# Folding a softmax scale, evicting two PSUM banks in one copy, and warming TensorE: one change of five parts to a packed attention and MLP kernel

## The chip, the cores and the metric

The kernel runs on one core of a Trainium2 chip. The metric is device time in microseconds (us), the median of several executions. The profile is taken in one execution; its span is 1.7 to 2.1 us shorter than the device time of that execution, so spans are compared with spans and times with times.

Engine names in the profile: PE is the matmul engine (TensorE), PEld its weight loads, DVE is VectorE, ACT is ScalarE, POOL is GpSimd, SP is the engine whose queue issues the stores. To evict means to copy a result from PSUM, where TensorE writes it, to SBUF. A "wall" is here an event, such as the landing of a load, before which a stage cannot begin.

Tile names: `a` or `a1` holds the weights of the first softmax, `a1T` their transpose, `a2u` the exponentials of the second softmax, `lns` the logarithms of its sums, `a2n` its normalised weights, `cosT` the cosine and `gT` the gated result.

## The reference

Two attentions follow one another, then an MLP with a cosine gate. There are 8 batches, 8 heads, 576 positions, a head size of 64, 32 "packed" queries, a model width of 512 and an inner width of 2048.

```python
def sm_attn(qq, kk, vv):
    s = scale * np.matmul(qq, kk.transpose(0, 1, 3, 2))
    a = softmax(s)                      # max subtracted, 1e-9 added to the sum
    return np.matmul(a, vv)
p_packed = sm_attn(p, k, v)             # 32 packed rows per head
out = sm_attn(q, p_packed, p_packed)    # every query looks at the 32 packed rows
x = out as (batch*576, 512)
h = x @ w_in
return (h * np.cos(h)) @ w_out
```

## The kernel before

The kernel never forms `x`. Because `x = A2 @ p_packed`, it multiplies the packed rows by `w_in` first (`PPW`, 256 rows by 2048 columns per batch, in four tiles of 512 columns) and then computes `h` as `A2 @ PPW`. The first softmax is not normalised when it is computed: its sums (the key sums) become a factor `r1` per packed row, which is applied when `PPW` is evicted from PSUM.

```python
def ppw(b, n, engs, pool=A):                    # tile n of packed-times-w_in
    ...
    t = psa(); ps = [t[:, 0, :], t[:, 1, :]]    # two PSUM banks of one tile
    for x in range(4):
        for y in range(2):
            nc.tensor.matmul(ps[y][32 * x:32 * x + 32, :], ppT[b % 2][r, 2 * x + y, :], w_in_bf[...])
    for y in range(2):                          # engs is (V, ACT) nearly everywhere
        dst = PPW[b][:, y, n * 512:(n + 1) * 512]
        if engs[y] is ACT:
            ACT.activation(out=dst, in_=ps[y], func=AF.Copy, scale=r1[b][:, y:y + 1])
        else:
            V.tensor_scalar(out=dst, in0=ps[y], scalar1=r1[b][:, y:y + 1], op0=ALU.mult)

def normalise(b):                               # second softmax: a2n = a2u / sum
    for y in range(2):
        ACT.activation(out=lns[b][:, y], in_=lns[b][:, y], func=AF.Exp, scale=-1.0)
    for y in range(2):
        V.tensor_tensor(out=a2n[b][:, y], in0=a2u[b][:, y], in1=lns[b][:, y], op=ALU.mult)

def h_mm(b, fc):                                # one of 16 chunks of h (128 columns)
    ps = psa()                                  # pool A: three tiles of two banks
    for y in range(2):
        for e in range(2):
            nc.tensor.matmul(ps[:, e, 0:HS], PPW[b][:, y, ...], a2n[b][:, y, ...], start=(y == 0), stop=(y == 1))
    ACT.activation(out=csv, in_=ps[:, :, 0:HS], func=AF.Sin, bias=pihalf)
    # rest(): DVE multiplies psum by the cosine and writes gT
```

Each engine does its instructions in the order in which the program gives them. The order is made by hand. In `ppw`, batch 0 is an exception: its halves go each into a PSUM tile of its own (pool `O`). `fill(n)` puts n matmuls of the previous batch's output product (128x512, the "filler") into TensorE's order wherever the batch's own work would leave it waiting. `slot(s, ...)` runs the 16 h chunks of batch s, and between them the pack product `pp` and the four `ppw` tiles of the next batch.

```python
for s in range(2, B):
    set_filler(s - 1)
    s2(s); fill(7)                       # query scores, exponentials
    s1(s + 1); xbar(...); a1_xbar(s + 1) # key scores of the next batch; a1 transposed by DMA
    fill(3); sums2(s, 0); fill(4); sums2(s, 1); normalise(s); fill(11)
    slot(s, front(s + 1, 4))             # pp at chunk 4, ppw at 7, 9, 11, 13
```

Batch 0 has no filler. Batch 1's transposes are done by TensorE, and their PSUM results are copied by DVE, ACT and DVE in turn (those of `a1` by DVE and ACT). The loads are all issued at the start, in the order keys, values, queries of batch 0, `w_in` (two pieces), the pack rows of batches 1 to 7, `w_in` (two pieces), `w_out` (four pieces), keys, values, queries of batch 1, and so on.

The softmax here doesn't subtract the row's maximum and nothing guards it: scores larger than these inputs give would overflow.

## Time and profile before

The time was 278.81 us (278.59 to 280.82, 3 runs). The table cuts the span by the loads of ACT's function tables, which mark the stages well: the exponential set is loaded before each batch's softmax, the sine set before its h chunks. "Period" is from one batch's exponential load to the next.

| stage | span before, us | what fills it |
|---|---|---|
| start to batch 1's exponential set | 38.96 | batch 0 alone, no filler |
| from there to batch 1's sine set ("stage 2") | 20.33 | attention of batch 1, with batch 0's filler |
| from there to batch 2's exponential set ("slot 1") | 23.96 | h of batch 1, six `ppw` tiles |
| periods of batches 2, 4, 6 | 29.71, 30.80, 29.71 | 80 filler matmuls each |
| periods of batches 3, 5 | 29.36, 28.92 | 64 filler matmuls each |
| batch 7 and the rest | 45.15 | h of batch 7, 80 output matmuls, last stores |

Busy shares of the whole span, and the row of TensorE's granted clock in 40 slices (9 is full speed), from the page of the kernel before:

```profile
PE 244.3 (88%) x1996; PEld 130.9 (47%) x1996; DVE 158.3 (57%) x257; ACT 191.1 (69%) x296; POOL 53.2 (19%) x67
...
PEclk9999999999999999999999999999999999999997
```

TensorE is busy 88% of the span, but a mean over such different stages says little. The busy time by stage says more (columns: stretch, its length, then busy us and instruction count of PE, PEld, DVE, ACT, POOL, then clock, DMA share, GB/s). The four rows are stage 2, slot 1, and batches 3 and 6:

```profile
core 0: us, PE busy (x) PEld busy (x) DVE busy (x) ACT busy (x) POOL busy (x), PEclk, DMA share, GB/s
38.96:59.29 20.33, 18.54 (x236) 10.69 (x234) 11.02 (x21) 13.65 (x26) 6.99 (x7) 1.00 1.19 181
59.29:83.25 23.96, 18.10 (x172) 9.34 (x172) 17.26 (x27) 17.48 (x27) 3.47 (x6) 1.00 0.89 133
...
112.96:142.32 29.36, 26.95 (x237) 13.94 (x236) 17.70 (x28) 22.97 (x36) 6.38 (x7) 1.00 0.85 151
...
202.04:231.75 29.71, 29.02 (x228) 15.21 (x234) 17.46 (x28) 23.14 (x36) 4.09 (x4) 1.00 0.35 78
```

In batch 6 TensorE is busy 98% of the time, in batch 3 92%, and in slot 1 only 18.1 of 24.0 us, with DVE and ACT no fuller. Slot 1 is held by an order of waits and not by one engine. The group list shows which (columns: line, engine, operation, out<-in, shapes, count | busy us, mean ns | idle us before it <- what ended it):

```profile
L188 ACT ACTIVATE PPW<-psA,r 128x512 bf16<-128x512 f32 x28 | 19.2, 687 | 18.4 <-DVE PPW L190 18.4
...
L190 DVE TENSOR_SCALAR PPW<-psA,r 128x512 bf16<-128x512 f32 x28 | 20.8, 744 | 0.6 <-PE psA L183 0.5
...
L214 DVE TENSOR_TENSOR a2n<-a2u,lns 128x576 bf16<-128x576 bf16 x16 | 11.4, 755 | 12.8 <-ACT lns L212 12.8
```

ACT sat idle 18.4 us in front of its 28 halves of the eviction, and each time DVE's half ended the idle time. The two halves, which were meant to run side by side, ran one after the other. The totals of the waits (who waited for whom: us in all, times, longest):

```profile
ACT PPW L188 <- DVE PPW L190: 18.4, 28, 1.6
...
PE psA L226 <- DVE a2n L214: 3.8, 9, 2.2
...
PE psA L160 <- DMA a1T<-a: 2.9, 3, 1.4
```

One turn of this in slot 1, in the timeline (start us, duration, engine, instruction, idle before and its cause):

```profile
77.81 0.76 DVE L233 TENSOR_TENSOR gT<-psA,cosT 128x576 bf16<-128x576 f32 x1 [0.72 <-ACT cosT L230]
...
78.48 0.74 DVE L190 TENSOR_SCALAR PPW<-psA,r 128x512 bf16<-128x512 f32 x1
...
79.26 0.69 ACT L188 ACTIVATE PPW<-psA,r 128x512 bf16<-128x512 f32 x1 [0.58 <-DVE PPW L190]
79.85 0.73 ACT L230 ACTIVATE cosT<-psA,pihalf 128x576 bf16<-128x576 f32 x1
80.00 0.65 PE L226 MATMUL psA<-a2n,PPW 128*128 128x288 bf16 x4 [0.51 <-ACT PPW L188]
```

DVE multiplies gT (77.81), then evicts its half (78.48), then ACT evicts its half (79.26), then ACT makes the next cosine (79.85), on which the next gT waits; TensorE's next h chunk (80.00) waits for ACT's half as well, because it needs the PSUM tile. One such turn takes 2.8 us for two h chunks.

The start of the kernel, in the timeline, and the landing time of the load that was issued at 19.29 (last column of the DMA view: us from issue to landing):

```profile
7.78 2.10 PE L102 MATMUL psA<-ident,kbf 96*128 96x96 bf16 x24 [3.83 <-DMA kbf<-in_k_dram]
...
19.29 0.79 POOL L84 DMA_DIRECT2D kbf<-in_k_dram  x1 [2.16 <-PE psA L124]
...
23.75 5.50 PE L226 MATMUL psA<-a2n,PPW 128*128 128x288 bf16 x24 [2.18 <-DVE a2n L214]
...
39.82 1.46 PE L102 MATMUL psA<-ident,kbf 96*128 96x96 bf16 x24
```

```profile
kbf<-in_k_dram POOLq DMA_DIRECT2D x1, 576.0 KB, 20.2
```

Two things are read here. The first 24 h matmuls of 288 columns took 5.50 us, 229 ns each; in the raw trace they start 240 ns apart up to 28.2 us and, within a chunk, 122 ns apart later. TensorE ran at half speed until then, although the clock row shows 9 throughout: the trace's first clock record is one of full speed at 28.30 us, and the row counts time without a record as full speed. And the keys of batch 1, which the transposes at 39.82 need, landed at 19.29 + 20.2 = 39.5 us. The transposes show no wait for them: batch 0's own chain still ended last, with the keys 0.3 us ahead.

### The profile page before, as it was taken

The page shows a single profiled execution, that of the slowest core. Times are in us where ns is not written, and L with a number is a line of the kernel's source. Part 1 is how long each engine was busy: PE and PEld are TensorE (multiplying, and loading weights), DVE is VectorE, ACT ScalarE, POOL GpSimd, SP SyncE. Part 2 cuts the span into 40 slices and gives each one's busy share as a digit, 9 for nine tenths or more (in the row PEclk, how much of TensorE's full clock was granted, in tenths as well). Part 3 has the DMA queues.
Part 4 walks back from the last instruction along what each step waited for, and adds up shares of the span by engine and source line. Part 5 has one row for each costly group of instructions (what it writes and reads, how often), then busy time and mean ns, then how long its engine had stood idle before and what let it go on. Part 6 is the DMA issues. An engine that isn't in the chain of part 4 may idle for free.

```text
span 276.9 us, 5007 instructions
## 1 busy us (share of the span) xinstructions
PE 244.3 (88%) x1996; PEld 130.9 (47%) x1996; DVE 158.3 (57%) x257; ACT 191.1 (69%) x296; POOL 53.2 (19%) x67
## 2 busy tenths in 40 slices
PE   0786889977879999998899999989999999999992
PEld 0563455444424655455445555455445544565440
DVE  2348995447771677456663677267726765587100
ACT  1347984696679766995789577977797678876000
POOL 8432002610404120403031300411040000000000
PEclk9999999999999999999999999999999999999997
DMA  7999999999299999299919894989264202111222
GB/s 98 204 224 206 206 206 157 199 153 177 23 202 182 193 156 175 62 191 163 216 45 170 166 220 90 145 193 160 59 132 94 52 29 62 43 40 38 76 76 77
DMA packets 62759, 37.09 MB, mean 134 GB/s; under 512 B 35488, under 2 KB 58016, under 8 KB 62736
## 3 DMA queue, kind: packets, MB, share of 16 engines
q0 software_dynamic: 23168, 18.81, 45.1%
q1 hardware_dynamic: 39568, 17.96, 30.9%
q8 instruction: 15, 0.25, 0.4%
q14 instruction: 8, 0.07, 0.1%
HBM read 37.22 MB, written 9.44 MB: 169 GB/s over the span
## 4 chain that ended last, share of the span: by engine, by line
PE 54%; ACT 18%; DVE 16%; DMA 6%; issue 4%; SPq 0%; ACTq 0%; POOLq 0%
PE ot L261 28%; PE psA L226 14%; DVE gT L233 6%; ACT cosT L230 5%; DVE PPW L190 5%; DMA a1T<-a 4%; ACT PPW L188 3%; DVE a2n L214 3%; PE psA L160 3%; PE psA L102 2%; DMA kbf<-in_k_dram 2%; PE psA L124 2%; ACT lns L206 2%; ACT lns L212 2%; PE psA L204 2%
## 5 line engine op out<-in xcount | busy, mean ns | idle before, releaser
L261 PE MATMUL ot<-w_out_bf,gT 128*128 128x512 bf16 x512 | 132.6, 380 | 0.0
L233 DVE TENSOR_TENSOR gT<-psA,cosT 128x576 bf16<-128x576 f32 x128 | 95.7, 755 | 41.6 <-ACT cosT L230 40.2
L230 ACT ACTIVATE cosT<-psA,pihalf 128x576 bf16<-128x576 f32 x128 | 93.5, 741 | 20.4 <-PE psA L226 19.0
L226 PE MATMUL psA<-a2n,PPW 128*128 128x288 bf16 x512 | 86.2, 291 | 10.8 <-DVE a2n L214 3.8
L226 PEld LDWEIGHTS <-PPW 128*128 128x128 bf16 x512 | 50.5, 99 | 51.5 <-issue 19.2
L261 PEld LDWEIGHTS <-gT 128*128 128x128 bf16 x512 | 46.7, 98 | 42.3 <-issue 6.9
L237 POOL COPY joint<-gT 128x512 bf16<-128x512 bf16 x16 | 9.7, 612 | 124.8 <-DVE gT L233 124.8
L188 ACT ACTIVATE PPW<-psA,r 128x512 bf16<-128x512 f32 x28 | 19.2, 687 | 18.4 <-DVE PPW L190 18.4
L75 ACT COPY osb<-ot 128x512 f32<-128x512 f32 x18 | 10.5, 581 | 16.1 <-PE ot L261 16.0
L190 DVE TENSOR_SCALAR PPW<-psA,r 128x512 bf16<-128x512 f32 x28 | 20.8, 744 | 0.6 <-PE psA L183 0.5
L77 DVE COPY osb<-ot 128x512 f32<-128x512 f32 x18 | 12.3, 682 | 11.6 <-PE ot L261 11.6
L214 DVE TENSOR_TENSOR a2n<-a2u,lns 128x576 bf16<-128x576 bf16 x16 | 11.4, 755 | 12.8 <-ACT lns L212 12.8
L77 POOL COPY vp<-vbf 96x3072 bf16<-96x3072 bf16 x6 | 16.5, 2749 | 0.0
L261 PE MATMUL ot<-w_out_bf,joint 128*128 128x512 bf16 x64 | 16.5, 380 | 0.0
L139 DVE RECIPROCAL r<-sums 128x2 f32<-128x2 f32 x8 | 1.3, 166 | 22.9 <-ACT a L133 22.9
L170 ACT CAST ppT<-psA 64x128 bf16<-64x128 f32 x16 | 4.2, 260 | 11.6 <-DVE ppT L166 9.8
L196 ACT ACTIVATE a2u<-psA,rs 128x576 bf16<-128x576 f32 x16 | 11.0, 737 | 1.2 <-PE psA L124 1.1
L183 PE MATMUL psA<-w_in_bf,ppT 64*32 64x512 bf16 x224 | 11.5, 386 | 0.3 <-DVE gT L233 0.2
L160 PE MATMUL psA<-a1T,vp 96*128 96x64 bf16 x192 | 7.5, 199 | 4.5 <-DMA a1T<-a 2.9
L133 ACT ACTIVATE a<-psA 128x576 bf16<-128x576 f32 x16 | 10.3, 652 | 1.7 <-PE psA L124 1.7
L206 ACT ACTIVATE lns<-psA 128x576 f32<-128x576 f32 x16 | 10.4, 659 | 1.2 <-PE psA L204 0.7
L84 POOL DMA_DIRECT2D kbf<-in_k_dram x8 | 6.3, 787 | 21.6 <-PE psA L102 18.6
(54 smaller groups left out, 154.5 us busy)
## 6 DMA issues: line engine op xcount, KB each, us to landing
kbf<-in_k_dram POOLq DMA_DIRECT2D x8, 576.0 KB, 11.5
vbf<-in_v_dram POOLq DMA_DIRECT2D x8, 576.0 KB, 7.0
qbf<-in_q_dram POOLq DMA_DIRECT2D x8, 576.0 KB, 9.4
out_dram<-osb SPq DMA_DIRECT2D x24, 192.0 KB, 2.5
out_dram<-osb SPq DMA_DIRECT2D x24, 128.0 KB, 2.4
w_in_bf<-in_moe_w_in_dram POOLq DMA_DIRECT2D x4, 512.0 KB, 15.4
w_out_bf<-in_moe_w_out_dram POOLq DMA_DIRECT2D x4, 512.0 KB, 20.4
out_dram<-osb SPq DMA_DIRECT2D x24, 64.0 KB, 2.1
```

Source lines behind the costliest of these rows:

```text
L77: eng.tensor_copy(out=out, in_=in_)
L160: nc.tensor.matmul(ps[:, 0, hp * 64:(hp + 1) * 64], vp[b][:, c, hp * 128:(hp + 1) * 128], a1T[b][0:TP, :, j, 32 * hp:32 * hp + 32], start= ...
L183: nc.tensor.matmul(ps[y][32 * x:32 * x + 32, :], ppT[b % 2][r, 2 * x + y, :], w_in_bf[r, x, n * 512:(n + 1) * 512], start=True, stop=True)
L188: ACT.activation(out=dst, in_=ps[y], func=AF.Copy, scale=r1[b][:, y:y + 1])
L190: V.tensor_scalar(out=dst, in0=ps[y], scalar1=r1[b][:, y:y + 1], scalar2=None, op0=ALU.mult)
L196: ACT.activation(out=a2u[b][:, y].rearrange("p (e x) -> p e x", e=2), in_=ps[y][:, :, 0:HS], func=AF.Exp, scale=rs1[b][:, y:y + 1])
L206: ACT.activation(out=lns[b][:, y].rearrange("p (e x) -> p e x", e=2), in_=ps[:, :, 0:HS], func=AF.Ln)
L214: V.tensor_tensor(out=a2n[b][:, y], in0=a2u[b][:, y], in1=lns[b][:, y], op=ALU.mult)
L226: nc.tensor.matmul(ps[:, e, 0:HS], PPW[b][:, y, fc * 128:(fc + 1) * 128], a2n[b][:, y, e * HS:(e + 1) * HS], start=(y == 0), stop=(y == 1))
L230: ACT.activation(out=csv, in_=ps[:, :, 0:HS], func=AF.Sin, bias=pihalf)
L233: V.tensor_tensor(out=gT[b][:, fc, :].rearrange("p (e x) -> p e x", e=2), in0=ps[:, :, 0:HS], in1=csv, op=ALU.mult)
L261: nc.tensor.matmul(ps, w, w_out_bf[:, fc, :], start=(fc == 0), stop=(fc == NFC - 1))
```

## The change

The intent was to take work off DVE and ACT in the slots and to keep TensorE busy and warm. It has five parts: (1) the key-sum scale `r1` moves from the eviction of `PPW` to the query normalisation, so that a `PPW` tile (two banks) can be evicted in one copy, by DVE and ACT in turn, with batch 0's tiles now in the shared pool too (the result is the same, since `r1` belongs to the packed row over which `h` sums); (2) 25 warm-up matmuls on zeros in batch 0; (3) the transposes of batch 1, the first ones of batch 2 and those of `a1` in batch 0 evicted by DVE alone; (4) other positions: fill counts 8, 4, 5, 13 in place of 7, 3, 4, 11, the pack product at chunk 5 in place of 4, two of batch 2's `ppw` tiles from slot 1 to slot 2, the packing of `p` in two parts; (5) the last output chunk in two halves, stored from two queues.

```diff
-    def ppw(b, n, engs, pool=A):
+    def ppw(b, n):
...
-        for y in range(2):
-            dst = PPW[b][:, y, n * 512:(n + 1) * 512]
-            if engs[y] is ACT:
-                ACT.activation(out=dst, in_=ps[y], func=AF.Copy, scale=r1[b][:, y:y + 1])
-            else:
-                V.tensor_scalar(out=dst, in0=ps[y], scalar1=r1[b][:, y:y + 1], scalar2=None, op0=ALU.mult)
+        copy((V, ACT)[n % 2], PPW[b][:, :, n * 512:(n + 1) * 512], ps)
...
-            V.tensor_tensor(out=a2n[b][:, y], in0=a2u[b][:, y], in1=lns[b][:, y], op=ALU.mult)
+            V.scalar_tensor_tensor(out=a2n[b][:, y], in0=a2u[b][:, y], scalar=r1[b][:, y:y + 1],
+                                   in1=lns[b][:, y], op0=ALU.mult, op1=ALU.mult)
...
+    def warm(n):
+        for _ in range(n):
+            nc.tensor.matmul(wps, wz[:, 0:128], wz, start=True, stop=True)
...
-            copy((V, ACT)[y], t[0:TP, y]..., ps[0:TP, 0, 0:C * 128])      # a1 of batches 1, 2 (and 0)
+            copy(V, t[0:TP, y]..., ps[0:TP, 0, 0:C * 128])
-            copy(ACT if i == 1 else V, t[:, 8 * i:8 * i + 8]..., ps[:, 0, 0:8 * TP])
+            copy(engs[i], ...)                                            # engs=(V, V, V); batch 0 (V, ACT, V)
...
+    warm(7)
     dup_p(0, 2)
     pack_p(0, 1)
-    pe_T("k", 0)
+    warm(9)
+    pe_T("k", 0, (V, ACT, V))
...  # warm(3) before a1 of batch 0, warm(6) after its normalise
-    for n in range(4):
-        for fc in range(4 * n, 4 * n + 4):
-            h_mm(0, fc)()
-            if fc == 4 * n + 1 and n in (1, 2):
-                ppw(0, n + 1, (V, ACT), O)
+    for fc in range(NFC):
+        h_mm(0, fc)()
+        if fc in (2, 6):
+            ppw(0, 2 + fc // 4)
+        if fc == 10:
+            pack_p(1, 3)
...
-    slot(1, [(1, ppw(1, 2)), (5, ppw(1, 3))] + front(2, 6), ...)          # abridged
+    slot(1, [(1, pw(1, 2)), (4, pw(1, 3)), (7, lambda: pp(2)), (9, lambda: pack_p(3, B)),
+             (11, pw(2, 0)), (14, pw(2, 1))], ...)
...
-        fill(7)
+        fill(8)
...
-        fill(3)
+        fill(4)
         sums2(s, 0)
-        fill(4)
+        fill(5)
         sums2(s, 1)
         normalise(s)
-        fill(11)
+        fill(13)
...
-        slot(s, front(s + 1, 4) if nxt else [], [])
+        pieces = [(1, pw(2, 2)), (4, pw(2, 3))] if s == 2 else []
+        if nxt:
+            pieces += [(5, lambda: pp(s + 1))] + [(8 + 2 * n, pw(s + 1, n)) for n in range(4)]
+        slot(s, pieces, [])
...
+    tail_chunk(B - 1, 4)      # last 128 rows: two halves of 256 columns, stores on SP and ACT queues
```

More of the change, by code (lines that the diff above doesn't have):

```diff
@@ L69 @@
     srcs = {"k": k, "q": q, "v": v}
-    bf, vp, xT, a1T, r1, rs1 = {}, {}, {}, {}, {}, {}
+    bf, vp, xT, a1T, sums1, r1, rs1 = {}, {}, {}, {}, {}, {}, {}
     a2u, lns, a2n, PPW = {}, {}, {}, {}
@@ L93, in xbar, with pe_T @@
         nc.sync.dma_start_transpose(out=t, in_=bf[n, b].rearrange("p h x -> p (h x)"))
-    def pe_T(n, b):
+    def pe_T(n, b, engs=(V, V, V)):
         t = xT[n, b] = att_pool.tile([128, H * 3, TP], BF16, name=n + "T", tag=n + "T")
@@ L103, in pe_T @@
                                     ident[0:TP, 0:TP])
-            copy(ACT if i == 1 else V, t[:, 8 * i:8 * i + 8].rearrange("p a x -> p (a x)"),
+            copy(engs[i], t[:, 8 * i:8 * i + 8].rearrange("p a x -> p (a x)"),
                  ps[:, 0, 0:8 * TP])
@@ L136, in s1, with recips @@
                 func=AF.Exp, scale=scale, accum_out=sm[:, y:y + 1])
+        sums1[b] = sm
+    def recips(b):
         r1[b] = small.tile([128, 2], FP32, name="r1")
         rs1[b] = small.tile([128, 2], FP32, name="rs1")
-        V.reciprocal(r1[b], sm)
+        V.reciprocal(r1[b], sums1[b])
         V.tensor_scalar(out=rs1[b], in0=r1[b], scalar1=scale, scalar2=None, op0=ALU.mult)
@@ L152, in a1_pe @@
                 nc.tensor.transpose(ps[0:TP, 0, c * 128:(c + 1) * 128], a1[b % 2][:, y, c, 0:TP], ident)
-            copy((V, ACT)[y], t[0:TP, y].rearrange("p c x -> p (c x)"), ps[0:TP, 0, 0:C * 128])
+            copy(V, t[0:TP, y].rearrange("p c x -> p (c x)"), ps[0:TP, 0, 0:C * 128])
     def pp(b):
@@ L170, in pp @@
             ACT.copy(out=t[z, :, y, :], in_=pv[r, :, y, :])
-    def ppw(b, n, engs, pool=A):
+    def ppw(b, n):
         if b not in PPW:
             PPW[b] = ppw_pool.tile([128, 2, DF], BF16, name="PPW", tag="PPW")
-        if pool is O:
-            ps = [O.tile([128, 512], FP32, name="ppw", tag="ot") for _ in range(2)]
-        else:
-            t = psa()
-            ps = [t[:, 0, :], t[:, 1, :]]
+        ps = psa()
         for x in range(4):
@@ L182, in ppw @@
                 r = slice(64 * y, 64 * y + 64)
-                nc.tensor.matmul(ps[y][32 * x:32 * x + 32, :], ppT[b % 2][r, 2 * x + y, :],
+                nc.tensor.matmul(ps[32 * x:32 * x + 32, y, :], ppT[b % 2][r, 2 * x + y, :],
                                  w_in_bf[r, x, n * 512:(n + 1) * 512], start=True, stop=True)
-        for y in range(2):
-            dst = PPW[b][:, y, n * 512:(n + 1) * 512]
-            if engs[y] is ACT:
-                ACT.activation(out=dst, in_=ps[y], func=AF.Copy, scale=r1[b][:, y:y + 1])
-            else:
-                V.tensor_scalar(out=dst, in0=ps[y], scalar1=r1[b][:, y:y + 1], scalar2=None, op0=ALU.mult)
+        copy((V, ACT)[n % 2], PPW[b][:, :, n * 512:(n + 1) * 512], ps)
     def s2(b):
@@ L254, in pieces_of, with n_chunks, tail_chunk @@
         return res
+    def n_chunks(b):
+        return 5 if b % 2 and b < B - 1 else 4
+    def tail_chunk(b, c):
+        osb = o_pool.tile([128, DM], FP32, name="osb")
+        for i in range(2):
+            cols = slice(i * 256, i * 256 + 256)
+            ps = O.tile([128, 256], FP32, name="ot", tag="ot")
+            for fc in range(NFC):
+                nc.tensor.matmul(ps, joint[b // 2][:, fc, :], w_out_bf[:, fc, cols],
+                                 start=(fc == 0), stop=(fc == NFC - 1))
+            copy((ACT, V)[i], osb[:, cols], ps)
+            for (a, z, rows), q in zip(pieces_of(b, c), (nc.sync, nc.scalar)):
+                q.dma_start(out=rows[:, cols], in_=osb[a:z, cols])
     def out_gen(b):
-        for c in range(5 if b % 2 else 4):
+        for c in range(n_chunks(b)):
             ps = O.tile([128, DM], FP32, name="ot", tag="ot")
@@ L275, in set_filler @@
         filler[0] = out_gen(b)
-        filler[1] = 16 * (5 if b % 2 else 4)
+        filler[1] = 16 * n_chunks(b)
     def fill(n):
@@ L294, in dup_p, with load_w_in, load_w_out @@
             V.tensor_copy(out=p_bf[:, a:b, t, :], in_=p_raw[:, a:b, :])
+    def load_w_in(n):
+        G.dma_start(out=w_in_bf[:, :, n * 512:(n + 1) * 512],
+                    in_=moe_w_in.rearrange("(a p) n -> p a n", p=128)[:, :, n * 512:(n + 1) * 512])
+    def load_w_out(n):
+        G.dma_start(out=w_out_bf[:, n * 4:(n + 1) * 4, :],
+                    in_=moe_w_out.rearrange("(a p) n -> p a n", p=128)[:, n * 4:(n + 1) * 4, :])
+    def dup_p(a, b):
+        for t in range(2):
+            V.tensor_copy(out=p_bf[:, a:b, t, :], in_=p_raw[:, a:b, :])
+    def warm(n):
+        for _ in range(n):
+            nc.tensor.matmul(wps, wz[:, 0:128], wz, start=True, stop=True)
     nc.sync.dma_start(out=p_raw[:, 0:2, :], in_=p_rows[:, 0:2, :])
@@ L313 @@
     load("q", 2)
+    wz = const.tile([128, 512], BF16, name="wz")
+    wps = O.tile([128, 512], FP32, name="wps", tag="ot")
+    V.memset(wz, 0.0)
     ACT.preload_act_table_set(EXP_SET)
@@ L320 @@
         V.memset(t[:, :, :, TP:128], 0.0)
+    warm(7)
     dup_p(0, 2)
     pack_p(0, 1)
-    pe_T("k", 0)
+    warm(9)
+    pe_T("k", 0, (V, ACT, V))
     s1(0)
     permute_v(0, V)
+    warm(3)
     a1_pe(0)
+    recips(0)
     pp(0)
-    pe_T("q", 0)
+    pe_T("q", 0, (V, ACT, V))
     s2(0)
-    ppw(0, 0, (V, V), O)
+    ppw(0, 0)
     sums2(0, 0)
     sums2(0, 1)
-    ppw(0, 1, (V, V), O)
+    ppw(0, 1)
     normalise(0)
+    warm(6)
     dup_p(2, 16)
-    for n in range(4):
-        for fc in range(4 * n, 4 * n + 4):
-            h_mm(0, fc)()
-            if fc == 4 * n + 1 and n in (1, 2):
-                ppw(0, n + 1, (V, ACT), O)
+    for fc in range(NFC):
+        h_mm(0, fc)()
[3 more added lines that the diff above has]
+            pack_p(1, 3)
     set_filler(0)
-    pack_p(1, 8)
     ACT.preload_act_table_set(EXP_SET)
@@ L352 @@
     a1_pe(1)
+    recips(1)
     fill(4)
@@ L356 @@
     fill(3)
-    ppw(1, 0, (V, ACT))
+    ppw(1, 0)
     s2(1)
@@ L360 @@
     pe_T("k", 2)
-    ppw(1, 1, (V, ACT))
+    ppw(1, 1)
     fill(3)
@@ L370 @@
     a1_pe(2)
+    recips(2)
     load("k", 3)
@@ L383, in slot, with pw @@
             fill((left * (fc + 1)) // NFC - done)
-    def front(b, fc0):
-        return [(fc0, lambda: pp(b))] + [(fc0 + 3 + 2 * n, lambda n=n: ppw(b, n, (V, ACT))) for n in range(4)]
+    def pw(b, n):
+        return lambda: ppw(b, n)
     def begin_loads(b):
@@ L395 @@
     xbar("k", 3)
-    slot(1, [(1, lambda: ppw(1, 2, (V, ACT))), (5, lambda: ppw(1, 3, (V, ACT)))] + front(2, 6),
-         [(8, lambda: begin_loads(3))])
+    slot(1, [(1, pw(1, 2)), (4, pw(1, 3)), (7, lambda: pp(2)), (9, lambda: pack_p(3, B)),
+             (11, pw(2, 0)), (14, pw(2, 1))], [(8, lambda: begin_loads(3))])
     for s in range(2, B):
@@ L412 @@
             a1_xbar(s + 1)
+            recips(s + 1)
             G.tensor_copy(out=gate, in_=a1T[s + 1][0:1, 0, 0, 0:1])
-        fill(3)
+        fill(4)
         sums2(s, 0)
-        fill(4)
+        fill(5)
         sums2(s, 1)
         normalise(s)
-        fill(11)
+        fill(13)
         for n, b in (("v", s + 2), ("q", s + 2), ("k", s + 3)):
```

## The prediction

> **What bounds the kernel.** Span 276.9 us; four limits (timeline, busy time by window).
>
> 1. 0 to 39.5 us: a serial chain for batch 0 on a slow TensorE: around 24.4 us fourteen 288-column matmuls took 3.53 us (252 ns each), later four take about 0.5. But the DMA queues are saturated too (205 to 222 GB/s): the key load of batch 1, issued at 19.29 us, landed 20.2 us later, at 39.5; its transposes start at 39.6.
> 2. 39 to 59 us: TensorE 18.1 of 19.9 us busy, ACT 88% at the end.
> 3. 59 to 83 us (slot 1): TensorE only 18.5 of 24.4 us, DVE 17.7, ACT 17.9. The waits and the chain name the packed-times-w_in eviction: ACT's half starts only after DVE's (18.4 us of ACT idle, 28 times), and the next matmul waits for ACT's.
> 4. 83 to 254 us: six periods. Batches 2, 4, 6 (80 filler matmuls) take 29.7, 30.8, 29.7 us, TensorE about 98% busy; batches 3 and 5 (64) 29.4 and 28.9, TensorE about 92%, waiting for the a1 DMA transpose (0.9 to 1.4 us in batches 3, 4, 5) and evictions. Then 18 us of output matmuls, and 4.9 us to the end.
>
> **Costs.**
> - Eviction: per tile DVE 744 + ACT 687 ns in series becomes one 1024-column copy. Estimate: the 512-column copies (DVE 682, ACT 581 ns) plus 512 columns at 0.96 and 1.2 GHz (the Trainium skill, "ScalarE: Activation LUTs" and "VectorE: DVE Perf Modes"): DVE 1.22 or ACT 1.01 us. Per batch 0.55 us less DVE, 0.7 less ACT, no series.
> - The scale moves into the a2n product: 755 to about 820 ns, 16 times: at most 1 us, mostly hidden.
> - Warm-up: "TensorE: Matmul & The Clock Gate" (Part 1) says about 3.4 us of matmuls lift the clock from 1.2 to 2.4 GHz. The cold parts (24 key transposes 2.10 us against 1.5 later; pack product 1.44 against 0.86; 12 a1 transposes 1.51 against 0.83) shrink; batch 0's first h matmuls start 2 to 2.5 us earlier, about 21.3. The third w_in piece lands only at 23.9, so its product may stall. Batch 0 then ends near 37.5 and waits for the keys at 39.5: the warm-up earns almost nothing, about 0.3 us.
> - Batch 1 transposes on DVE: five ACT copies of 0.80 us become 0.55 us each on DVE; with the shorter evictions stage 2 is about 1 us shorter.
> - Slot 1 loses two of six w_in products (to slot 2, TensorE-bound, +0.7 us) and the series: 24 to about 19.5 us, -4.5.
> - Five more fillers ahead of each slot and the pack product one step later take away the a1 wait; with shorter evictions batches 3 and 5 gain 1.6 each, batch 4 1.1, batch 6 0.1, batch 7 nothing.
> - Tail: 256-column copy, half-size stores on two queues: -0.6.
>
> Sum: -0.3 -1.0 -4.5 +0.7 -4.3 -0.1 -0.6 = about -10.
>
> **Predicted time 268.7 us**, 8 in 10 between 264.5 and 273. Faster by over 2%: 0.86; within 2%: 0.12; slower: 0.02.
>
> **What would show it.** First h matmul near 21.3 us, 24 key transposes in 1.5 us (warm-up); batch 1's first key transposes still near 39.5 (DMA wall); slot 1 about 19.5 us, no ACT wait on DVE's eviction; evictions 1.0 and 1.2 us; no pack-product wait for a1; batches 2 and 6 near 29.7 to 30.4.
>
> **What would make it wrong.** Keys landing before 39.5 (up to 2 us more); the clock not rising before the keys land, or cold warm-up matmuls delaying them; slot 1 held by its three PSUM buffers and strict order above 21 us; loads for batch 3 late once slot 1 is short; a slower a2n product delaying each first h matmul.

## The result, and the profile after

The changed kernel is correct. Its time is 264.78 us (264.67 to 265.36, 4 runs); the kernel before took 278.70 us in the same rounds (278.20 to 280.82, 4 runs, the three quoted above and one more). The ratio is 0.9495, with a 95% interval from 0.9451 to 0.9539.

```profile
PE 244.6 (93%) x2037; PEld 132.1 (50%) x2037; DVE 158.5 (60%) x248; ACT 182.7 (69%) x276; POOL 53.5 (20%) x67
...
PEclk9997999999999999999999999999999999999998
```

TensorE's busy time is the same as before (244.6 us) in a span that is 13.9 us shorter. The clock row now dips in its fourth slice, which is treated below. Busy time by stage, the same four stages and columns:

```profile
38.19:56.47 18.28, 16.78 (x228) 10.04 (x228) 10.48 (x20) 9.75 (x19) 6.98 (x7) 1.00 1.25 194
56.47:76.73 20.26, 18.21 (x173) 10.07 (x170) 17.55 (x28) 15.69 (x22) 2.97 (x5) 1.00 0.93 149
...
106.70:133.23 26.53, 26.45 (x237) 14.12 (x236) 17.49 (x26) 22.59 (x34) 6.38 (x7) 1.00 0.93 167
...
190.05:218.93 28.88, 28.51 (x221) 15.22 (x219) 17.48 (x26) 22.45 (x34) 4.09 (x4) 1.00 0.39 81
```

```profile
L208 DVE SCALAR_TENSOR_TENSOR a2n<-a2u,r,lns 128x576 bf16<-128x576 bf16 x16 | 12.4, 815 | 20.1 <-ACT lns L206 20.1
...
L77 DVE CAST PPW<-psA 128x1024 bf16<-128x1024 f32 x16 | 19.5, 1220 | 1.5 <-PE psA L182 1.2
L75 ACT CAST PPW<-psA 128x1024 bf16<-128x1024 f32 x16 | 16.1, 1005 | 2.6 <-PE psA L182 2.6
```

The 16 copies on each engine took 1220 ns (DVE) and 1005 ns (ACT) for 1024 columns; the prediction had estimated 1.22 and 1.01 us. The normalisation's product rose from 755 to 815 ns. The waits that answer to those of before:

```profile
ACT PPW L75 <- PE psA L182: 2.6, 2, 1.5
...
PE psA L102 <- DMA kbf<-in_k_dram: 1.2, 2, 0.9
...
PE psA L221 <- DVE a2n L208: 0.8, 3, 0.3
```

The wait of ACT's half for DVE's is gone, since no tile has two halves. There is no longer a wait of the pack product for the a1 transpose, and the wait for the normalised queries (`a2n`) fell from 3.8 to 0.8 us. Slot 1 now, around a tile that ACT evicts in one piece:

```profile
74.00 1.46 DVE L228 TENSOR_TENSOR gT<-psA,cosT 128x576 bf16<-128x576 f32 x2 [0.19 <-ACT cosT L225]
...
74.57 1.00 ACT L75 CAST PPW<-psA 128x1024 bf16<-128x1024 f32 x1
74.81 0.65 PE L221 MATMUL psA<-a2n,PPW 128*128 128x288 bf16 x4 [0.21 <-DVE gT L228]
```

DVE makes two products of gT (74.00) while ACT evicts (74.57); the next h chunk waits only 0.21 us. The start of the kernel:

```profile
7.40 1.19 PE L102 MATMUL psA<-ident,kbf 96*128 96x96 bf16 x24 [0.34 <-DMA kbf<-in_k_dram]
...
17.34 0.40 PE L198 MATMUL psA<-a2u,ones_blk 128*128 128x288 bf16 x2 [0.23 <-ACT a2u L190]
...
19.23 0.63 PE L182 MATMUL psA<-w_in_bf,ppT 64*32 64x512 bf16 x8 [1.50 <-DMA w_in_bf<-in_moe_w_in_dram]
...
19.80 2.74 PE L320 MATMUL wps<-wz 128*128 128x512 bf16 x6
19.93 1.01 ACT L75 CAST PPW<-psA 128x1024 bf16<-128x1024 f32 x1 [1.51 <-PE psA L182]
...
20.84 1.26 ACT L206 ACTIVATE lns<-lns 128x576 f32<-128x576 f32 x2
...
22.44 0.48 PE L221 MATMUL psA<-a2n,PPW 128*128 128x288 bf16 x2
...
39.11 1.19 PE L102 MATMUL psA<-ident,kbf 96*128 96x96 bf16 x24 [0.86 <-DMA kbf<-in_k_dram]
```

The first key transposes take 1.19 us in place of 2.10, and the trace's first record of full clock is at 5.56 us in place of 28.30, so the warm-up worked. But the key transposes of batch 1 start at 39.11, after a wait for the DMA, where they started at 39.82 before. The key load was issued at 19.76 and landed 19.3 us later, at 39.1.

The whole difference by stage, with the prediction's terms beside it:

| stage | before | after | difference | predicted |
|---|---|---|---|---|
| start to batch 1's exponential set | 38.96 | 38.19 | -0.77 | -0.3 |
| stage 2 | 20.33 | 18.28 | -2.05 | -1.0 |
| slot 1 | 23.96 | 20.26 | -3.70 | -4.5 |
| batch 2 | 29.71 | 29.97 | +0.26 | +0.7 |
| batch 3 | 29.36 | 26.53 | -2.83 | -1.6 |
| batch 4 | 30.80 | 29.54 | -1.26 | -1.1 |
| batch 5 | 28.92 | 27.28 | -1.64 | -1.6 |
| batch 6 | 29.71 | 28.88 | -0.83 | -0.1 |
| batch 7 and the rest | 45.15 | 44.07 | -1.08 | -0.6 |
| span | 276.9 | 263.0 | -13.9 | -10.1 |

### The profile page after: what moved, and what is told of

Its sections match the earlier page's. It is cut to its first block, busy times and chain, and to the rows that moved or that the text cites. A ratio compares the mean times of both kernels' runs of the same rounds, so it can differ in the third digit from the quotient of the medians.

```text
span 263.0 us, 5065 instructions
## 1 busy us (share of the span) xinstructions
PE 244.6 (93%) x2037; PEld 132.1 (50%) x2037; DVE 158.5 (60%) x248; ACT 182.7 (69%) x276; POOL 53.5 (20%) x67
## 4 chain that ended last, share of the span: by engine, by line
PE 66%; DMA 13%; ACT 9%; DVE 7%; issue 2%; POOL 1%; DVEq 0%; ACTq 0%; POOLq 0%
PE ot L271 39%; PE psA L221 17%; DMA kbf<-in_k_dram 7%; DMA w_in_bf<-in_moe_w_in_dram 5%; DVE gT L228 4%; ACT cosT L225 3%; PE psA L182 2%; PE psA L163 2%; DVE PPW L77 2%; ACT PPW L75 1%; ACT L438 1%; PE psA L124 1%; PE ot L260 1%; PE psA L198 1%; PE psA L102 1%
## 5 line engine op out<-in xcount | busy, mean ns | idle before, releaser
L221 PE MATMUL psA<-a2n,PPW 128*128 128x288 bf16 x512 | 83.4, 285 | 5.5 <-DVE gT L228 3.1
L208 DVE SCALAR_TENSOR_TENSOR a2n<-a2u,r,lns 128x576 bf16<-128x576 bf16 x16 | 12.4, 815 | 20.1 <-ACT lns L206 20.1
L77 DVE COPY osb<-ot 128x512 f32<-128x512 f32 (+1 forms) x19 | 12.7, 670 | 15.1 <-PE ot L271 12.0
L75 ACT COPY osb<-ot 128x512 f32<-128x512 f32 (+1 forms) x18 | 10.3, 574 | 15.0 <-PE ot L271 10.1
L77 DVE CAST PPW<-psA 128x1024 bf16<-128x1024 f32 x16 | 19.5, 1220 | 1.5 <-PE psA L182 1.2
L75 ACT CAST PPW<-psA 128x1024 bf16<-128x1024 f32 x16 | 16.1, 1005 | 2.6 <-PE psA L182 2.6
L182 PE MATMUL psA<-w_in_bf,ppT 64*32 64x512 bf16 x256 | 13.4, 393 | 2.2 <-DMA w_in_bf<-in_moe_w_in_dram 1.5
L271 PE MATMUL ot<-w_out_bf,joint 128*128 128x512 bf16 x48 | 12.9, 380 | 0.0
L320 PE MATMUL wps<-wz 128*128 128x512 bf16 x25 | 9.4, 537 | 1.2 <-DVE wz L342 1.2
```

The lines of the kernel that those rows point to most:

```text
L75: ACT.copy(out=out, in_=in_)
L77: eng.tensor_copy(out=out, in_=in_)
L182: nc.tensor.matmul(ps[32 * x:32 * x + 32, y, :], ppT[b % 2][r, 2 * x + y, :], w_in_bf[r, x, n * 512:(n + 1) * 512], start=True, stop=True)
L208: V.scalar_tensor_tensor(out=a2n[b][:, y], in0=a2u[b][:, y], scalar=r1[b][:, y:y + 1], in1=lns[b][:, y], op0=ALU.mult, op1=ALU.mult)
L221: nc.tensor.matmul(ps[:, e, 0:HS], PPW[b][:, y, fc * 128:(fc + 1) * 128], a2n[b][:, y, e * HS:(e + 1) * HS], start=(y == 0), stop=(y == 1))
L271: nc.tensor.matmul(ps, w, w_out_bf[:, fc, :], start=(fc == 0), stop=(fc == NFC - 1))
```

## The experiments

Twelve kernels ran, all correct, in three sets of four, each set on one chip. The theory to be tested was the one of the prediction: the gain comes from the eviction without its series and from the a1 wait that goes away, and the warm-up earns nothing because a load of batch 1 is a wall. The rivals stand in the expectations. The kernel before took 278.52, 279.08 and 278.57 us beside the three sets, so it moved by 0.56 us between sets; the changed kernel ran in none of them. A difference of about half a microsecond from its 264.78 us is therefore not shown by the times alone, and the stage spans below are the better witness. Stage spans (same cuts as above) of the first six:

| stage | after | e1 | e2 | e3 | e4 | e5 | e6 |
|---|---|---|---|---|---|---|---|
| start | 38.19 | 40.51 | 40.80 | 38.36 | 39.71 | 38.66 | 38.34 |
| stage 2 | 18.28 | 17.49 | 18.64 | 18.04 | 19.31 | 18.51 | 18.10 |
| slot 1 | 20.26 | 20.26 | 21.71 | 20.25 | 21.44 | 20.06 | 22.31 |
| batch 2 | 29.97 | 29.97 | 30.40 | 30.61 | 29.52 | 29.97 | 28.88 |
| batch 3 | 26.53 | 26.53 | 27.77 | 28.00 | 28.38 | 26.54 | 26.56 |
| batch 4 | 29.54 | 29.54 | 29.54 | 30.65 | 30.74 | 29.53 | 29.54 |
| batch 5 | 27.28 | 27.13 | 27.45 | 28.22 | 28.13 | 27.53 | 27.45 |
| batch 6 | 28.88 | 28.88 | 29.16 | 29.52 | 29.52 | 28.88 | 28.88 |
| rest | 44.07 | 44.09 | 43.83 | 44.55 | 45.35 | 44.12 | 44.14 |

### e1: no warm-up

```diff
     def warm(n):
-        for _ in range(n):
-            nc.tensor.matmul(wps, wz[:, 0:128], wz, start=True, stop=True)
+        return
```

> The changed kernel without any of its 25 warm-up matmuls, else the same. Theory (DMA wall): batch 1's first key transposes stand near 39 us with or without them, because the key load lands at 39; the time rises by 0.0 to 0.8 us over the changed kernel's 264.8 (the first h matmul falls back to 23.5 or later, the key transposes stay within 0.6 us of 39.1). Rival (the warm-up is a main part of the gain): 267 us or more, with the key transposes of batch 1 over 1.5 us later.

Measured: 266.35 us (266.14 to 266.45), ratio 0.9558 [0.9541, 0.9576]. That is 1.6 us above the changed kernel, between the theory and the rival. The key transposes of batch 1 began at 40.42, 1.3 us later. Batch 0 ended 2.3 us later without the warm-up (40.51 against 38.19), and stage 2 gave 0.8 us of it back (17.49 against 18.28), because in the changed kernel stage 2 begins with the wait for the keys. The wall is there and takes a third of the warm-up's lead, but not all of it. From slot 1 to the end the two kernels agree to 0.2 us.

The reason that the prediction had a lower figure is the kernel that it compared with: batch 0's chain in e1 is itself slower than that of the kernel before (the transposes began at 40.42 against 39.82). The warm-up is worth 1.6 us in the changed kernel, of which 0.6 us only make up for that.

### e2: two halves per tile

```diff
-        copy((V, ACT)[n % 2], PPW[b][:, :, n * 512:(n + 1) * 512], ps)
+        for y in range(2):
+            copy((V, ACT)[y], PPW[b][:, y, n * 512:(n + 1) * 512], ps[:, y, :])
```

> The changed kernel, scale still folded into the query normalisation, but each packed-times-w_in tile copied again in two 512-column halves, y=0 by DVE and y=1 by ACT. Theory (the series of the two halves was the cost): ACT's half again waits for DVE's (18 us of ACT idle in all) and most of what the slots gained is lost: 4 to 7 us slower than 264.8, slot 1 near 23 us. Rival (the gain came from the moved pieces and fill counts, or from the scale leaving the eviction): within 1.5 us of 264.8.

Measured: 271.44 us (270.67 to 271.90), ratio 0.9739 [0.9715, 0.9763], 6.7 us slower than the changed kernel. The theory holds as to the total and the wait, which is back with the scale still folded away:

```profile
ACT PPW L75 <- DVE PPW L77: 21.6, 31, 2.3
```

So the single copy counts, and not the scale's leaving the eviction as such. The place was only partly right: slot 1 is 21.7 us, not 23; batch 3 loses 1.2 us; and 2.6 us are lost in batch 0, which the expectation had not named. There TensorE also fell back to its low clock: from 31 to 40 us the granted clock was 0.81 (1.00 in the changed kernel), and its last 20 h matmuls took 4.35 us. In the 3.41 us before that fall, at 35.56 us, TensorE was busy for 1.83 us; that the slower h chunks brought it about is likely but not shown.

### e3: the old fill counts and positions

```diff
-        fill(8)
+        fill(7)
-        fill(4) ... fill(5) ... fill(13)
+        fill(3) ... fill(4) ... fill(11)
-            pieces += [(5, lambda: pp(s + 1))] + [(8 + 2 * n, pw(s + 1, n)) for n in range(4)]
+            pieces += [(4, lambda: pp(s + 1))] + [(7 + 2 * n, pw(s + 1, n)) for n in range(4)]
```

> The changed kernel with the old fill counts of batches 2 to 7 (7, 3, 4, 11 in place of 8, 4, 5, 13) and the pack product and w_in products one h chunk earlier (4; 7, 9, 11, 13), as before. Theory: the pack product again waits for the a1 DMA transpose in batches 3, 4, 5, about 1 us each: 2 to 3.5 us slower than 264.8. Rival: those waits are given back later in the slot by the filler, so under 1 us slower.

Measured: 270.04 us (269.85 to 270.87), ratio 0.9700 [0.9674, 0.9727], 5.3 us slower, far above both the theory's 2 to 3.5 us and the rival. The expectation failed. The waits of e3 name two causes and not one:

```profile
PE psA L163 <- DMA a1T<-a: 2.5, 3, 1.2
PE psA L221 <- DVE a2n L208: 2.5, 9, 0.3
```

The first is the a1 wait, 2.5 us, as expected. The second, the wait of h matmuls for the normalised queries, was not in the theory: 2.5 us against 0.8 in the changed kernel. It is paid in every period, also in batches 2 and 6, where no a1 wait is seen and which are 0.64 us longer in e3. The timeline shows how, at the first h chunk of batch 6 in e3, and then in the changed kernel:

```profile
200.85 0.41 PE L221 MATMUL psA<-a2n,PPW 128*128 128x288 bf16 x2
201.53 0.41 PE L221 MATMUL psA<-a2n,PPW 128*128 128x288 bf16 x2 [0.27 <-DVE a2n L208]
201.77 0.81 PE L271 MATMUL ot<-w_out_bf,gT 128*128 128x512 bf16 x3
```

```profile
197.63 0.66 PE L221 MATMUL psA<-a2n,PPW 128*128 128x288 bf16 x4
198.12 0.81 PE L271 MATMUL ot<-w_out_bf,gT 128*128 128x512 bf16 x3
```

`a2n` has two halves. In e3 TensorE has run out of filler when only the first is ready: two matmuls, a wait, two matmuls, 201.77 - 200.85 = 0.92 us for the chunk. With five fillers more ahead of it both halves are there, and the chunk takes 198.12 - 197.63 = 0.49 us. The raw trace shows the same in all six periods (0.92 to 0.93 us against 0.49 to 0.52). The fillers cost nothing, since they only leave the slot, where they would have been done later.

### e4: the kernel before with one part

The kernel before, with the single copy and the scale in the normalisation, and nothing else of the change (the diff is that of `ppw` and `normalise` above).

> The kernel before with one part of the change alone: the scale in the normalisation and one copy per packed-times-w_in tile (DVE and ACT in turn), old positions of all else. Theory (the series is the largest part): 271 to 274 us, that is 5 to 7.5 us off 278.7; slot 1 near 21.5 us; the a1 waits remain. Rival (the moved pieces matter more): 275.5 or more.

Measured: 274.11 us (273.96 to 274.62), ratio 0.9841 [0.9821, 0.9861]: 4.4 us gained, just short of the range of the theory (5 to 7.5). Slot 1 is 21.44 us, as expected, stage 2 gains 1.0 us, and batches 3 and 5 gain 1.0 and 0.8 us. Start loses 0.75 us: in batch 0 the second tile's copy falls to ACT, where it stands (1.01 us, at 21.57) between the logarithms and the exponentials, which begin at 22.47 in place of 21.49. The part is worth 4.4 us alone and 6.7 us as the last one taken away (e2). The two do not undo the same thing: e2 puts batch 0's halves into one PSUM tile, where the kernel before had two, and 2.6 of its microseconds are lost there.

### e5: ACT takes part in the transposes again

```diff
-    def pe_T(n, b, engs=(V, V, V)):
+    def pe_T(n, b, engs=(V, ACT, V)):
-            copy(V, t[0:TP, y]..., ps[0:TP, 0, 0:C * 128])
+            copy((V, ACT)[y], t[0:TP, y]..., ps[0:TP, 0, 0:C * 128])
```

> The changed kernel with the transposes of batch 1 (keys, queries, a1) and the second batch's keys and a1 copied by DVE, ACT, DVE (a1: DVE, ACT) again, as before. Theory: ACT gets five copies of 0.80 us back in the stage between the two exponential and sine table loads (18.3 us in the changed kernel), where DVE has room; the stage grows by 0.4 to 1.2 us and the time to 265.2 to 266.0. Rival: ACT is no longer near full there once the evictions are single copies (it was busy 9.8 of 18.3 us), so nothing changes: within 0.3 us.

Measured: 265.88 us (265.56 to 266.66), ratio 0.9541 [0.9520, 0.9562], 1.1 us slower: the theory, and not the rival. From the first key transposes of batch 1 to its sine set the two take 57.17 - 38.94 = 18.23 us (e5) and 56.47 - 39.11 = 17.36 us. So ACT mattered although it was busy only 9.8 of 18.3 us there: the share of a stage does not show which single copies are waited for. The edit does a little more than the expectation says: it also gives ACT one of batch 0's two `a1` copies. Batch 0 ended 0.5 us later in e5 (38.66 against 38.19), but the key transposes, at 38.94, still waited 0.21 us for the keys, which is why the stage is counted from them.

### e6: all six products in slot 1

```diff
-             (7, lambda: pp(2)), (9, lambda: pack_p(3, B)), (11, pw(2, 0)), (14, pw(2, 1))]
+             (7, lambda: pp(2)), (8, lambda: pack_p(3, B)), (9, pw(2, 0)), (11, pw(2, 1)), (13, pw(2, 2)), (15, pw(2, 3))]
-        pieces = [(1, pw(2, 2)), (4, pw(2, 3))] if s == 2 else []
+        pieces = []
```

> The changed kernel with all four packed-times-w_in tiles of batch 2 back in slot 1 (chunks 9, 11, 13, 15; the pack of the other batches at 8) and none in slot 2. Theory: slot 1 grows from 20.3 to about 22 us and batch 2's period shrinks from 30.0 to about 29.2 us, so 0.5 to 1.3 us slower in all. Rival: the single copies took the cost out of slot 1 already, so within 0.4 us.

Measured: 266.27 us (265.93 to 266.45), ratio 0.9550 [0.9533, 0.9566], 1.5 us slower, a little more than the theory's range. Slot 1 grew by 2.05 us and batch 2 shrank by 1.09 us. Two tiles cost 1 us in a stage that TensorE bounds, and 2 us in one that ACT and DVE bound in turn.

### e7: the late pack rows

```diff
-    G.dma_start(out=p_raw[:, 2:, :], in_=p_rows[:, 2:, :])
+    G.dma_start(out=p_raw[:, 2:6, :], in_=p_rows[:, 2:6, :])
...  # after load("q", 1)
+    G.dma_start(out=p_raw[:, 6:, :], in_=p_rows[:, 6:, :])
-    dup_p(2, 16)
+    dup_p(2, 6)
...  # just before slot 1
+    dup_p(6, 16)
```

> The changed kernel with only the pack rows of batches 1 and 2 loaded early (128 KB) and the other ten groups (320 KB) after batch 1's queries; their copy moves to just before slot 1. Nothing else is moved. Theory (DMA wall): at about 0.206 MB per us the keys of batch 1 land some 1.6 us earlier, at 37.5, and the time falls by 0.8 to 1.8 us, to 263.0 to 264.0. Rival (batch 0's own chain ends the prologue, not the DMA queues): within 0.3 us of 264.8.

Measured: 265.05 us (264.35 to 265.26), ratio 0.9503 [0.9483, 0.9522]: no gain, so the rival's number. Its profile shows why it is neither. The key transposes began at 38.39, 0.7 us earlier, and with no wait for the DMA; what held them now was batch 0's own chain, whose last product of gT had yet to begin, at 38.51. Stage 2 was left 0.49 us earlier than in the changed kernel (55.98 against 56.47). But slot 1 grew from 20.26 to 20.90 us, since the copies of the late rows (0.89 us of DVE) now stood at its head. There are two walls, one 0.7 us behind the other, and the edit paid for the first with a new cost.

### e8: the new fill counts with the old positions

```diff
-            pieces += [(5, lambda: pp(s + 1))] + [(8 + 2 * n, pw(s + 1, n)) for n in range(4)]
+            pieces += [(4, lambda: pp(s + 1))] + [(7 + 2 * n, pw(s + 1, n)) for n in range(4)]
```

> The changed kernel with its own fill counts (8, 4, 5, 13) but the pack product and w_in products one h chunk earlier (4; 7, 9, 11, 13) as before. The run with both undone was 5.3 us slower, of which its waits for the a1 transpose are 2.5 us. Theory (two effects: the fillers cover the time in which TensorE waits for the normalised queries; the place covers the a1 transpose): waits of about 0.9 us come back in batches 3 and 5, none in 2 and 4: 1.2 to 2.4 us slower than 264.8. Rival (the place is the whole of it): 4 us or more. Rival (the fillers are the whole of it): under 0.6 us.

Measured: 266.77 us (266.19 to 267.37), ratio 0.9567 [0.9541, 0.9593], 2.0 us slower than the changed kernel: inside the theory's range, outside both rivals'. Its wait:

```profile
PE psA L163 <- DMA a1T<-a: 1.8, 2, 1.2
```

Of e3's 5.3 us, 2.0 are lost with the old position alone, and 3.3 more with the old fillers (270.04 - 266.77). The traces account for the 3.3 roughly: six first chunks, each about 0.42 us longer, are 2.5 us, the a1 waits are 0.7 us longer in e3 than in e8 (2.5 against 1.8), and so are TensorE's waits for the exponentials of the query scores, which stand before the second half of the key scores (1.7 against 0.9). These terms sum to more than 3.3, so the shares are not exact. No run has the old fillers with the new position.

### e9: the queries of batch 0 earlier

```diff
     sums2(0, 1)
-    ppw(0, 1)
     normalise(0)
...
-    dup_p(2, 16)
     for fc in range(NFC):
         h_mm(0, fc)()
-        if fc in (2, 6):
-            ppw(0, 2 + fc // 4)
+        if fc in (1, 5, 8):
+            ppw(0, 1 + fc // 3)
+        if fc == 6:
+            dup_p(2, 16)
```

> The changed kernel with batch 0's second w_in product (and its copy on ACT, which stood between the logarithm and the exponential and waited for the second w_in piece to land at 19.2 us) moved behind the normalisation, to h chunk 1, the third to 5, the fourth to 8, and the copy of the pack rows to 6. Nothing of the loads is moved. Theory (the key load of batch 1 is the wall): the first h matmul comes 1.5 to 2.5 us earlier, near 20.2, but the key transposes of batch 1 stay between 38.6 and 39.4 and the time within 0.6 us of 264.8. Rival (batch 0's chain is what counts): 1.2 us or more faster, the key transposes before 38.

Measured: 265.09 us (264.72 to 265.90), ratio 0.9518 [0.9482, 0.9554]: the theory. The first h matmul came 2.56 us earlier and the keys did not move:

```profile
19.88 0.40 PE L221 MATMUL psA<-a2n,PPW 128*128 128x288 bf16 x2 [0.87 <-DVE a2n L208]
...
39.07 1.19 PE L102 MATMUL psA<-ident,kbf 96*128 96x96 bf16 x24 [1.64 <-DMA kbf<-in_k_dram]
```

This is the clearest showing of the DMA wall. Batch 0's chain did not end 2.6 us earlier, since the product and the copy were moved to among its h chunks; it ended 0.83 us earlier (37.36 against 38.19). The wait for the keys grew by as much, from 0.86 to 1.64 us, and nothing came of it.

### e10 to e12: the loads in another order, with and without the earlier queries and the warm-up

```diff
 # e10; e11 = e10 and e9 together; e12 = e11 without the warm-up matmuls
-    G.dma_start(out=p_raw[:, 2:, :], in_=p_rows[:, 2:, :])
+    G.dma_start(out=p_raw[:, 2:6, :], in_=p_rows[:, 2:6, :])
     load_w_in(2)
     load_w_in(3)
+    load("k", 1)
     for n in range(4):
         load_w_out(n)
-    load("k", 1)
     load("v", 1)
     load("q", 1)
+    G.dma_start(out=p_raw[:, 6:, :], in_=p_rows[:, 6:, :])
...
     sums2(1, 1)
+    dup_p(6, 16)
     normalise(1)
```

> The changed kernel with the loads reordered only: keys of batch 1 ahead of the four w_out pieces, and the pack rows of batches 3 to 7 after batch 1's queries (their copy now just ahead of batch 1's normalisation, where DVE is idle, not in slot 1). Batch 0's chain is as in the changed kernel. In the run with the late pack rows the key transposes began at 38.4, behind batch 0's own chain. Theory: the same here, 38.0 to 38.5, and this time nothing lost in slot 1: 0.3 to 1.0 us faster than 264.8. Rival (DMA order alone is the wall): 1.5 us or more faster.

> Both of the edits of this set at once. Theory (two walls one behind the other, each of which hides the other): more than the sum of the two alone; the key transposes of batch 1 near 36.5, the time 1.5 to 2.8 us below 264.8, 262.0 to 263.3. Rival (the queries and values of batch 1, or TensorE itself between 39 and 56 us, are the next wall): no better than the run with the keys first.

> Both edits, without the 25 warm-up matmuls. Theory: with the wall gone, all of the warm-up's lead counts, 2.0 to 3.0 us slower than the run with both edits, where it was worth 1.6 us in the changed kernel. Rival (the warm-up's worth does not depend on the loads): 1.2 to 1.8 us slower.

| kernel | time, us | ratio to before | first h matmul | batch 1's key transposes |
|---|---|---|---|---|
| changed | 264.78 (264.67 to 265.36) | 0.9495 [0.9451, 0.9539] | 22.44 | 39.11 |
| e9, earlier queries | 265.09 (264.72 to 265.90) | 0.9518 [0.9482, 0.9554] | 19.88 | 39.07 |
| e10, keys first | 264.08 (263.83 to 264.60) | 0.9478 [0.9444, 0.9512] | 22.19 | 37.83 |
| e11, both | 263.49 (262.73 to 264.06) | 0.9453 [0.9416, 0.9489] | 20.25 | 36.97 |
| e12, both, no warm-up | 265.69 (265.63 to 266.52) | 0.9540 [0.9505, 0.9575] | 22.35 | 39.78 |

e10 gained 0.7 us, as the theory had it, though the keys came a little earlier than it said. e11 gained 1.3 us on the changed kernel, more than the sum of the two alone (0.3 lost and 0.7 gained). The key transposes say the same without the times: 0.04 and 1.28 us earlier alone, 2.14 us together, which is what two walls that hide one another do. In time, e11 is only 0.6 us below e10, and their ranges overlap. It missed its own range (1.5 to 2.8 us): the keys were transposed at 36.97 and not 36.5, and the values of batch 1 became the next wait (at 40.61 DVE had waited 1.39 us for them). e12 is 2.2 us slower than e11, so with the keys out of the way the warm-up is worth 2.2 us, where e1 gave 1.6 in the changed kernel. The theory's range holds, barely; a difference of 0.6 us between sets is at the edge of what can be told.

e11 is the fastest kernel. The changed kernel was not run in that set, so the 1.3 us between them are across sets; within the set, e11 is 1.6 us faster than e9, which differs from it only in the loads and the copies of the late pack rows.

## Why the prediction was right or wrong

The time was predicted as 268.7 us with a range from 264.5 to 273.0; it was 264.78. The direction and most mechanisms were right, the sum of the terms too small: 10 us in place of 13.9. The time lies only 0.28 us inside the lower end of the range, and errors of both signs are in the sum. Of the 3.8 us that are missing from it, 3.1 are in the periods from batch 2 to the end (7.4 us gained, 4.3 predicted).

**Right: the eviction.** The series of the two halves was the largest single item. Putting it back cost 6.7 us (e2) and it alone earned 4.4 (e4), with the wait named in the profile of before. The copies took what was estimated. The estimate used the clocks in the Trainium skill, "ScalarE: Activation LUTs" (What ACT_TABLE_LOAD costs), one element per cycle at 1.2 GHz, and in "VectorE: DVE Perf Modes" (The TRN2 errata), 0.96 GHz, to add 512 columns to the measured copies; this case's trace agrees (1005 and 1220 ns).

**Right: the DMA wall, with a wrong size beside it.** Batch 1's key transposes were to stay near 39.5 and were at 39.11; e9 shows that a batch 0 that ends 0.8 us earlier moves nothing. That the warm-up "earns almost nothing, about 0.3 us" was too strong. Taken away it costs 1.6 us (e1), because without it batch 0 lets the key transposes begin only at 40.42, 1.3 us later than with it.

**Wrong: the first h matmul near 21.3 us.** It came at 22.44. The step that failed is that the prediction looked only at the third `w_in` piece. The second lands at about 19.2, TensorE waits 1.5 us for it (the line at 19.23 above), and the tile's copy stands in ACT's order between the logarithm and the exponential (19.93, then 20.84). e9 moved it, and the first h matmul came at 19.88. At the end of the kernel this error was worth nothing.

**Wrong, and the largest term: the fillers.** The prediction costed "five more fillers ahead of each slot and the pack product one step later" only for the a1 wait and the shorter evictions, in batches 3, 4 and 5, and gave batch 6 0.1 us and batch 7 nothing. Together the two edits are worth 5.3 us (e3). About 2.0 us are the position (e8). The other 3.3 us are the fillers (e3 against e8): the largest share, about 2.5 us, is the wait for the second half of the normalised queries, in each of six periods, and the rest is more of the a1 wait and of the wait before the second half of the key scores. That TensorE would wait for `a2n` stood in the prediction only as a danger of the change ("a slower a2n product"), not as a cost that the fillers would remove. The split first chunk was in the profile of before as well (3.8 us of waits for `a2n`, nine times, of which 2.2 us are batch 0's single wait, so about 0.2 us each for the others); it was given no cost, and the changed product, which takes 815 ns in place of 755 per half, may have made it longer (0.27 to 0.28 us each in e3).

**Mis-sized: stage 2.** It was to gain 1.0 us and gained 2.05. e4 puts 1.0 us of it on the single copies, e5 0.9 us on the transposes' move to DVE, so each of the two was worth about what had been given to both.

**Mis-sized: slot 1.** 19.5 us was predicted and 20.26 measured; e6 shows that the two products moved out of it are worth 2.05 us there, and e2 puts 1.45 us on the copies.

**The tail** was to gain 0.6 us. From the last matmul to the end of the span it took 4.94 us before (276.9 - 271.96) and 4.05 after (263.0 - 258.95). This is read from the two traces; no run undid it alone.

The runs that undo one part sum to 1.6 + 6.7 + 5.3 + 1.1 + 1.5 = 16.2 us, and with the tail to 17, more than the 13.9 us in all. The parts overlap, and e2 loses 2.6 us in batch 0, where the kernel before had no such series.

**Why ACT's half waited for DVE's half** is answered in part by a comparison. Both halves were in one PSUM tile and one `PPW` tile. The Trainium skill, "PSUM — Partial Sum Buffer" (PSUM bank collisions raise a hardware error), forbids two engines on the same bank and group of 32 partitions at once. These halves were in different banks. In batch 0 of the kernel before, the halves of tiles 2 and 3 were in different banks as well, but each in a PSUM tile of its own, with one `PPW` tile for both:

```profile
29.97 0.69 ACT L188 ACTIVATE PPW<-ppw,r 128x512 bf16<-128x512 f32 x1
...
30.82 0.74 DVE L190 TENSOR_SCALAR PPW<-ppw,r 128x512 bf16<-128x512 f32 x1
```

ACT's half began first and did not wait for DVE's, here and in the next tile (33.61 before 34.43). In e2, where batch 0's halves share a PSUM tile, ACT waited for DVE in the same two places (1.49 us before 27.31, 1.42 us before 32.23). So the shared `PPW` tile does not force the order, and the shared PSUM tile goes with it. As the banks differ in both cases, an order put in by the program's dependency tracking is more likely than a limit of the chip.

**Left open.** No run gave each half a PSUM tile of its own outside batch 0. Two halves side by side are therefore an untested rival to the single copy.

## What to carry to other kernels

When two engines share an eviction, look in the waits whether one half begins only after the other; if it does, look first whether they share a PSUM tile; one wider copy by alternating engines was shorter here than two halves in series, and a per-row scale that stands in the way can often move to another operand. A speed-up of a prologue is worth only what the next load leaves of it: find the landing time of the first load behind it before costing a warm-up, and look for a second wall just behind the first. Work that can be done anywhere, such as the filler here, belongs ahead of the point where the critical operand arrives, and a wait of 0.4 us in each of six periods is worth more than two waits of a microsecond.

## What the Trainium skill lacked or had wrong

- "TensorE: Matmul & The Clock Gate" (Why this matters for your kernels) gives idle gaps of more than about 3 us as what drops the clock. In the changed kernel the longest gap near the drop was 1.5 us (17.74 to 19.23). The trace's clock record falls to half at 19.21 for 3.41 us; in the 3.41 us before, TensorE was busy for 1.22 us. The six 512-column matmuls after it took 2.74 us, 457 ns each. In e9, which has no such wait there, the clock does not fall. The page's "A second HAM failure mode" does tell of short idle times that lower the clock, but gives no length. Two of the changed kernel's four runs have mean clocks of 0.999 and 1.000, so hardly any drop, and are not faster (264.75 and 265.36 us). From 19.7 to 26.3 us the granted clock was 0.78, the third figure from the end of this row of the changed kernel's busy time by stretch:

```profile
19.70:26.30 6.60, 5.46 (x38) 2.62 (x31) 4.54 (x7) 5.45 (x7) 2.33 (x3) 0.78 1.24 206
```

- The same page (Part 4) says that full clock does not engage for transposes. Here 24 transposes took 2.10 us before and 1.19 us after warm-up matmuls, so they do run faster once the clock is up. Its 3.4 us of matmuls to lift the clock (Part 1), which the prediction used, was a little short here: the warm-up began at 1.20 us and the clock record rises at 5.56, 4.4 us later. The transition that the page observed around 4 us fits better. The nine matmuls from 4.37 us on took 2.70 us, where the pace of the first seven would give 4.1 (3.17 / 7 x 9).
- "ScalarE: Activation LUTs" (What ACT_TABLE_LOAD costs) puts a table switch at about 2.66 us, load and drain. The load takes 1.28 us, as the page has it, and the next activation follows at once: in the kernel before, load at 202.04, activation at 203.33. No drain was seen, and ACT's idle time before its eight loads of the sine set was 0.1 us in all.
- The first page (Part 1) warns that clock events in a trace can be unreliable, but not that the time before the first of them can be shown as full speed: in the kernel before, the clock row shows 9 in the slices up to 28 us, where h matmuls start 240 ns apart, and the first clock record is at 28.30 us.
